# Attention and channel mix on one core: value loads on 128 partitions, products by even and odd key blocks, five turned batches, four loads in flight

## The chip, the cores and the metric

One core of a Trainium2 chip runs the whole kernel. The metric is the device time of one execution in microseconds, as the median of some runs. TensorE is called PE in the profile, VectorE DVE, ScalarE ACT, GpSimd POOL and SyncE SP.

## What is computed

Eight batches of causal attention, with 8 heads, 576 positions and 64 columns a head. The mask works by blocks of 64 positions, so query block i sees key blocks 0 to i whole. The heads' outputs, side by side, make x of 512 columns, which goes through a channel mix:

```python
attn = softmax(where(block_i >= block_j, q @ k.T / 8, -1e9));  x = heads_side_by_side(attn @ v)
x_prev = x shifted by one position
xk = mu_k * x + (1 - mu_k) * x_prev;  xr = mu_r * x + (1 - mu_r) * x_prev
out = sigmoid(xr @ w_r) * (relu(xk @ w_k) ** 2 @ w_v)
```

w_k is 512 x 1024, w_v 1024 x 512, w_r 512 x 512. Inputs and output are float32; the kernel computes products in 16 bits.

## The kernel before, in words

**Tasks and order.** The kernel first lists some 980 tasks, each with an engine, the tasks that it depends on and the buffers that it uses. Then it issues them in an order that is written out by hand: ORDER is a list of task numbers, and each engine works through its own tasks in that order, one after the other. A "+n" behind a number asks for n fills ahead of that task: matmuls of the identity (`unread`, L252, 128x512) whose result nobody reads, and which keep TensorE busy while it would wait. PLACE says, with one letter for each task that may go to several engines, which one takes it. Both texts are replaced by the change.

**Loads and their queue.** SP issues all transfers in its own order: loads (`load`, L224), turns (L349) and stores (L824). A transfer that has to wait holds all that stand behind it. Loads of float32 go into a ring of seven buffers (`ld`) and are cast to 16 bits on POOL, DVE or ACT (`convert`, L235 to L243).

**q and k.** Scores need q and k with the 64 columns of a head on partitions. In the first batches ("long", LONGS = 4: batches 0 to 3), a load brings two heads by two (`longld`, runs of 2,304 bytes, 576 KB a load; halves in batch 0). After the cast (`long`), TensorE transposes (`qt`, L302, 18 transposes of 64x64 a task, 8 tasks a batch, written into one bank of PSUM by both halves of the array), and ACT or DVE copies the result to SBUF (`ev`, 4 a batch). In the later batches a load brings 128 positions by 64 columns (`qkld`, in two pieces of 288 KB, runs of 256 bytes), and after the cast (`qk`) a transposing transfer (`turn`, L349) writes the turned form; there are four turns a batch, and all four must have landed ahead of the first scores.

**Attention.** `sc b gi` computes a unit of scores, keys on partitions: 12 units a batch, 14 in batch 0. Each unit writes a buffer of ring `s` in PSUM (three buffers of two banks). `ex` (ACT, L458) takes the exponential into ring `e`. Half u of the partitions holds the heads 4u to 4u + 3; c counts the four heads in a half. Then `av` multiplies by the values with column tiles of 32 and row tiles of 64: task S adds up the exponentials by a matrix of ones, `pick` (L488), A and B give the even and the odd columns of the output (L497, 72 matmuls each), T the first 64 queries (16 matmuls, into the same PSUM buffer as S). The order was S, T, A, B or another mixture; none waits for another. In A and B, row half u always writes bank u. DVE turns the sums (`t1`, L531), takes reciprocals (`rec`) and spreads them (`t2`), and `norm` (L560, L552) multiplies each product by them into x. Batch 0 goes through attention in two parts (L591, L596), the first 256 queries ahead; there A and B of the first part lie in one buffer, X.

**Values.** `vld b g` loads 64 positions on partitions: heads 0 to 3 on partitions 0 to 63 and heads 4 to 7 on 64 to 127, as two transfers of 64 partitions each (288 KB, runs of 256 bytes). `v` casts them to ring `vo`.

**Mix.** `d` (POOL or DVE) subtracts neighbours, `mul` (DVE, L686) makes xk and xr. In chunks of 512 positions, `pk` (L733) multiplies by w_k, `relu` and `sq` square it, `pr` (L768) multiplies by w_r, `tanh` stands for the sigmoid, `pv` (L799) multiplies by w_v, and `o` (DVE, L811) makes the output in a ring of two `o` buffers, whose `store` goes out through SP. pk, pr and pv share a ring of two banks (`mm`).

Of the kernel before, what the change touches and what calls it, by code (L numbers as in the profile page):

```python
# [9 lines left out]
F16 = mybir.dt.float16  # L10
# [4 lines left out]
LONGS = 4  # L15

ORDER = """
# [54 lines left out]
    "PPDDPDPPDDPPPAAPDAAAAAADPPDDDDPPDAPPDDADAADDPPPPAPPPDAAAPPDDDAPDAA"  # L72
    "ADDDDDDDPAPAPPPDDPDDDPDPDDDDDAAADDDDDPPDPDDDPPDDAAAPDPDPAPDPAADAAA"
    "DADADADADPAPAPDDAPADAADAAAADAADPDDAPAPAPAADAAAADDAAAAPAAAPDAAAAAAA"
    "DDAAAADPAAAPADDPADADAPADAAAPADADADAPAAAPAPADADAPAPADAPAPADAA")
# [56 lines left out]
def kernel(  # L132
# [64 lines left out]
    pick = consts.tile([P, QC], F16)  # L197
# [9 lines left out]
    for u in range(2):  # L207
        nc.vector.memset(
            pick[u * D:u * D + D, u * QC // 2:(u + 1) * QC // 2], 1.0)
# [3 lines left out]
    tiles, cast, evac = {}, {}, {}  # L213

# [5 lines left out]
    def load(key, dst_key, buf, jobs):  # L220
        def fn(eng, me):
            tiles[dst_key] = new(buf)
            for dst, src in jobs(tiles[dst_key]):
                nc.sync.dma_start(dst, src)  # L224
        return add(key, "SP", fn, uses=[buf])
# [95 lines left out]

    def add_cross(b):
# [5 lines left out]
        for g in range(2):  # L328
            for n, src in enumerate((q, k)):
# [4 lines left out]
                             (d[:, x].rearrange("p (i c) -> p i c", c=D),  # L334
                              src[b, 4 * g + 2 * x:4 * g + 2 * x + 2]
                              .rearrange("h s c -> (h s) c").rearrange(
                                  "(i p) c -> p i c", p=P))
# [23 lines left out]
    def operand(b, it, y, x, n):  # L361

        at = (it + 2 * y if b < LONGS else 2 * y + it) * S
        return new(qkt_buf[b])[x * D:x * D + D, n, at:at + S]

    def values(b):
        return new(vo_buf[b])[:, :].rearrange(
            "p (c t d) -> p c t d", c=4, d=D)

    def add_v(b):  # L370
        for g in range(2):
            vl = plan.buf("ld")
            t = load(f"vld {b} {g}", ("vl", b, g), vl, lambda d, g=g: [
                (d[u * D:u * D + D].rearrange("p x (t d) -> p (x t) d", d=D),
                 v[b, 4 * u + 2 * g:4 * u + 2 * g + 2].rearrange(
                     "x (t p) d -> p (x t) d", p=D))
                for u in range(2)])

            def fn(eng, me, g=g):
                convert(eng, new(vo_buf[b])[:, 2 * S * g:2 * S * (g + 1)],  # L380
                        tiles["vl", b, g][:, :].rearrange("p x c -> p (x c)"))
            cast["v", b, g] = flex(f"v {b} {g}", ANY, fn, [t],
                                   uses=[vl, vo_buf[b]])

# [50 lines left out]
    def add_scores(b, it):  # L435
# [5 lines left out]
        def fn(eng, me):  # L441
            PS = new(m)
            unread(me, PS[:, 0])
            for col, t, q0, n in UNITS[b][it[1]]:
                for y in range(2):
                    for x in range(2):
                        nc.tensor.matmul(  # L447
                            PS[y * D:y * D + D, x, col:col + n],
                            operand(b, it[0], y, x, 1)[:, t * D:t * D + D],
                            operand(b, it[0], y, x, 0)[:, q0:q0 + n],  # L450
# [14 lines left out]
    def weight(vals, kind):  # L465
        f = "AB".index(kind)
        return values(vals[0])[vals[1], vals[2], vals[3]].rearrange(
            "p (c f) -> p f c", f=2)[:, f]

    HALF = S // 2  # L470

    def blocks(b, PA, kind):

        for t in ([JT] * (kind in "ST") + [*range(JT)] * (kind != "T")):
# [3 lines left out]
            for c in range(GH):  # L480
# [3 lines left out]
                if kind == "S":  # L484
                    for y in range(2):
                        a, z = max(lo, y * HALF), min(lo + n, (y + 1) * HALF)
                        if a < z:
                            nc.tensor.matmul(  # L488
                                PA[out, y, a - y * HALF:z - y * HALF], pick,
# [4 lines left out]
                for u in range(2):  # L494
                    rows = slice(u * D, u * D + D)
                    for f in range(2) if kind == "T" else ("AB".index(kind),):
                        nc.tensor.matmul(  # L497
                            PA[out, u, HALF + f * D:HALF + f * D + D]
                            if kind == "T" else PA[out, u, lo - D:lo - D + n],
                            weight((b, rows, c, t % JT), "AB"[f]),  # L500
                            E[rows, bank, at:at + n],
                            start=t in (0, JT), stop=t >= JT - 1)

    def add_av(b):
# [3 lines left out]
        vals = [cast["v", b, g] for g in range(2)]  # L508
# [4 lines left out]
        for kind in "STAB":  # L513
            tail = kind == "T"

            def fn(eng, me, kind=kind):
                PA = new(m[kind])
                unread(me, PA[:, 0])
                blocks(b, PA, kind)
# [390 lines left out]
```

## Time and profile before

| what | value |
|---|---|
| median of 3 runs | 264.09 us (264.03 to 264.37) |
| the profiled execution | 266.22 us |
| its span, from first to last instruction | 264.4 us |
| mean clock granted to TensorE | 0.992 |
| HBM read, written | 33.56 MB, 9.44 MB |
| packets of the data queue q1 | 106,432, of which 95,040 under 512 bytes |
| SP: store L824 waited for DVE (o) | 72.2 us in total |
| ACT: exponentials waited for scores | 21.3 us in total |

The page of the profile gives busy times by engine, a view in 40 slices of the span (a digit is the busy share in tenths), the DMA queues, the chain of work that ended last, followed back from the end, and groups of instructions by line. The trace answers finer questions: who waited for whom, the chain in order of time, the busy time in chosen windows, the queue of SP. A line of the chain has its start in us, its length in us, the engine, the tile that it writes, the line of the kernel and the number of instructions. A line of a window has the window, its length, then for PE, PEld, DVE, ACT and POOL the busy time and the number of instructions, then the clock granted to TensorE, the DMA share and GB/s.

### The profile page before, as it was taken

To read this page: it belongs to the slowest core of one execution; us is meant where nothing else is said; L and a number is where in the kernel's file an instruction comes from. 1 tells how busy PE (TensorE), PEld (TensorE's weight loads), DVE (VectorE), ACT (ScalarE), POOL (GpSimd) and SP (SyncE) were. 2 spreads that over 40 slices of the span, in tenths; PEclk is the share of its full clock that TensorE was granted. 3 is DMA by queue.
4 is the path that set the end of the run, shared out by engine and by line. 5 is a ranking of instruction groups with operands and counts; after the bars stand their busy time and mean duration, and the time that the engine had idled before them with its cause. 6 is when DMAs were issued, how large, how long until landed. Compare 5 with 4: busy or idle time off the path is not lost.

```text
span 264.4 us, 8844 instructions
## 1 busy us (share of the span) xinstructions
PE 249.4 (94%) x3916; PEld 127.2 (48%) x3916; DVE 182.7 (69%) x270; ACT 178.8 (68%) x241; POOL 71.7 (27%) x71
## 2 busy tenths in 40 slices
PE   7899677996999999999999999979999999999994
PEld 3555346764446444554554455435544464444452
DVE  0448636889497987799858968957699578743332
ACT  1779587893799689598499855976688540472530
POOL 3215544442407511122144013001310324130410
PEclk9999999999799999999999999999999999999999
DMA  7999999399999999999789999999602200300403
GB/s 227 275 250 390 389 202 319 119 333 206 214 195 299 205 151 263 243 191 198 154 225 197 178 227 190 188 258 218 154 0 82 79 5 26 134 2 0 159 21 139
DMA packets 106470, 48.28 MB, mean 183 GB/s; under 512 B 95040, under 2 KB 95296, under 8 KB 106432
## 3 DMA queue, kind: packets, MB, share of 16 engines
q1 hardware_dynamic: 106432, 47.72, 79.1%
q8 instruction: 30, 0.49, 0.9%
q14 instruction: 8, 0.07, 0.1%
HBM read 33.56 MB, written 9.44 MB: 163 GB/s over the span
## 4 chain that ended last, share of the span: by engine, by line
PE 91%; issue 3%; ACT 2%; DMA 2%; DVE 1%; POOL 0%; SPq 0%; POOLq 0%; DVEq 0%; ACTq 0%
PE t_mm L733 24%; PE t_mm L799 24%; PE t_mm L768 11%; PE t_s L447 9%; PE t_s L497 7%; PE t_mm L252 6%; PE t_s L302 4%; PE t_s L488 4%; DMA out_dram<-t_o 2%; PE t_s L596 1%; ACT t_e L458 1%; PE t_s L591 1%; ACT t_qkt L235 0%; DVE t_o L811 0%; ACT t_kr L744 0%
## 5 line engine op out<-in xcount | busy, mean ns | idle before, releaser
L458 ACT ACTIVATE t_e<-t_s 128x1024 f16<-128x1024 f32 (+3 forms) x98 | 88.5, 957 | 21.6 <-PE t_s L447 21.3
L733 PE MATMUL t_mm<-t_xk,WK 128*128 128x512 f16 (+1 forms) x320 | 68.9, 358 | 1.4 <-issue 1.4
L799 PE MATMUL t_mm<-WV,t_k 128*128 128x512 f16 (+1 forms) x296 | 67.2, 380 | 1.6 <-DVE t_o L811 1.6
L755 POOL TENSOR_TENSOR t_k<-t_kr 128x512 f16<-128x512 f32 x27 | 29.6, 1104 | 101.6 <-ACT t_kr L744 55.3
L744 ACT ACTIVATE t_kr<-t_mm 128x512 f32<-128x512 f32 x53 | 31.5, 598 | 22.3 <-PE t_mm L733 21.6
L799 PEld LDWEIGHTS <-t_k 128*128 128x128 f16 x296 | 28.6, 99 | 35.6 <-issue 4.4
L733 PEld LDWEIGHTS <-WK 128*128 128x128 f16 x320 | 29.3, 98 | 31.6 <-issue 5.3
L811 DVE SCALAR_TENSOR_TENSOR t_o<-t_t,t_mm 128x512 f32<-128x512 f32 (+1 forms) x37 | 24.8, 671 | 22.7 <-PE t_mm L799 17.9
L768 PE MATMUL t_mm<-WR,t_xr 128*128 128x512 f16 x144 | 35.8, 380 | 0.2 <-ACT t_kr L744 0.2
L778 ACT ACTIVATE t_t<-t_mm 128x512 f32<-128x512 f32 x36 | 21.6, 601 | 15.7 <-PE t_mm L768 15.4
L447 PE MATMUL t_s<-t_qkt 64*64 64x512 bf16 (+7 forms) x680 | 30.0, 283 | 0.7 <-ACT t_qkt L235 0.7
L686 DVE SCALAR_TENSOR_TENSOR t_xr<-t_d,MUR,t_xt 128x576 f16<-128x576 f32 (+4 forms) x44 | 28.0, 650 | 2.4 <-POOL t_d L664 2.3
L686 DVE SCALAR_TENSOR_TENSOR t_xk<-t_d,MUK,t_xt 128x576 f16<-128x576 f32 (+4 forms) x44 | 29.2, 686 | 0.2
L241 POOL CAST t_nl<-t_ld 128x1152 bf16<-128x1152 f32 (+1 forms) x17 | 18.0, 1071 | 39.6 <-DMA t_ld<-in_k_dram 20.6
L447 PEld LDWEIGHTS <-t_qkt 64*64 64x64 bf16 x680 | 14.6, 106 | 17.3 <-issue 13.0
L755 DVE TENSOR_TENSOR t_k<-t_kr 128x512 f16<-128x512 f32 x17 | 13.3, 793 | 12.6 <-ACT t_kr L744 12.4
L753 ACT ACTIVATE t_k<-t_kr 128x512 f16<-128x512 f32 x28 | 17.2, 630 | 6.2 <-PE t_mm L799 6.0
L768 PEld LDWEIGHTS <-t_xr 128*128 128x128 f16 x144 | 13.0, 98 | 16.3 <-issue 2.8
L252 PE MATMUL t_mm<-identb 128*128 128x512 bf16 x59 | 17.4, 410 | 3.6 <-issue 2.2
L497 PE MATMUL t_s<-t_e,t_vo 64*32 64x512 f16 (+7 forms) x1120 | 20.6, 284 | 0.0
L664 POOL TENSOR_TENSOR t_d<-t_xt 128x576 f32<-128x576 f32 (+2 forms) x13 | 14.3, 1108 | 22.7 <-DVE t_xt L552 10.8
L560 DVE TENSOR_TENSOR t_xt<-t_s,t_rt 128x1024 f32<-128x1024 f32 x14 | 17.1, 1222 | 4.8 <-PE t_s L497 4.3
(47 smaller groups left out, 192.8 us busy)
## 6 DMA issues: line engine op xcount, KB each, us to landing
t_ld<-in_v_dram SPq DMA_DIRECT2D x32, 288.0 KB, 6.6
out_dram<-t_o SPq DMA_DIRECT2D x17, 512.0 KB, 3.6
t_ld<-in_q_dram SPq DMA_DIRECT2D x20, 288.0 KB, 5.4
t_ld<-in_k_dram SPq DMA_DIRECT2D x20, 288.0 KB, 5.1
t_ld<-in_k_dram SPq DMA_DIRECT2D x6, 576.0 KB, 7.0
t_ld<-in_q_dram SPq DMA_DIRECT2D x6, 576.0 KB, 6.4
t_ld<-in_moe_w_k_dram SPq DMA_DIRECT2D x4, 512.0 KB, 9.1
t_ld<-in_moe_w_v_dram SPq DMA_DIRECT2D x4, 512.0 KB, 6.4
```

The source lines that it names most:

```text
L252: nc.tensor.matmul(spare.get("at", dst), identb, identb[:, :].unsqueeze(1).to_broadcast([P, 4, P]), start=True, stop=True)
L447: nc.tensor.matmul(PS[y * D:y * D + D, x, col:col + n], operand(b, it[0], y, x, 1)[:, t * D:t * D + D], operand(b, it[0], y, x, 0)[:, q0:q ...
L458: nc.scalar.activation(new(ebuf)[:, :, 0:w], new(m)[:, :, 0:w], AF.Exp, scale=ISQ)
L497: nc.tensor.matmul(PA[out, u, HALF + f * D:HALF + f * D + D] if kind == "T" else PA[out, u, lo - D:lo - D + n], weight((b, rows, c, t % JT ...
L686: nc.vector.scalar_tensor_tensor(around[name][:, cc, at:at + w], new(d)[:, lo:lo + w], (MUK1, MUR1)[n][:, cc:cc + 1], x, ALU.mult, ALU.add)
L733: nc.tensor.matmul(ps[:, n], WK[:, cc, jc * P:(jc + 1) * P], xk[:, cc, lo:lo + w], start=(cc == 0), stop=(cc == CCn - 1))
L744: nc.scalar.activation(new(kr), new(m), AF.Relu)
L755: (nc.vector if eng == "DVE" else nc.gpsimd).tensor_tensor(dst, KR, KR, ALU.mult)
L768: nc.tensor.matmul(new(m), xr[:, cc, jt * P:(jt + 1) * P], WR[:, cc], start=(cc == 0), stop=(cc == CCn - 1))
L778: nc.scalar.activation(new(tb), new(m), AF.Tanh, scale=0.5)
L799: nc.tensor.matmul(new(m)[:, 0:w], k2[:, jc, jt * P:(jt + 1) * P], WV[:, jc, lo:lo + w], start=(jc == 0), stop=(jc == JCn - 1))
L811: nc.vector.scalar_tensor_tensor(new(o)[:, u, lo:lo + w], new(tiles["tbf", c, jt])[:, lo:lo + w], 1.0, new(m)[:, 0:w], ALU.add, ALU.mult)
```

## The change

- **Turned batches.** LONGS is 3: batch 3's q and k are now loaded in 256-byte runs and turned by transfers; its eight `qt` and four `ev` tasks go, four `turn` tasks come.
- **Values.** A value load brings 128 positions on partitions by blocks of 64 columns, two heads in a piece, as q and k are loaded in later batches. So a key block t of head c in half u stands on the upper or the lower 64 partitions by whether 9c + t + u is even. The load of the second half begins one block earlier, and the last block of head 7 of each batch, which no piece holds, comes for all batches by one more load (`vtld`) and cast (`vt`).
- **Products.** Row tiles must match the partitions of the values. So the scores of block t write the half that its values have (in `add_scores`, `u = y ^ t & 1 ^ ...`), and `pick` gets a second form for the odd blocks. An output is now added up by one row half over even blocks and by the other over odd blocks. `av` is split accordingly: A multiplies all even blocks (both column sets), then S, then T, then B with all odd blocks. S waits for A, T for `t1` (the turned sums of S), B for T, and all norms but T's for B. In batch 0 the first part too has A, S and B, with A and B in two buffers; B waits for `t1` and begins with one small matmul of 128 rows.
- **Loads in flight.** From the 13th to the 48th load transfer, a load waits until the fourth before it has landed.
- **Order.** ORDER and PLACE are new: 973 tasks, and 63 fills instead of 60. Batch 1's q and k are loaded ahead of batch 0's values. No task changes its sizes but as told.

```diff
-LONGS = 4
+LONGS = 3
...
+                ins = nc.sync.dma_start(dst, src).ins
+                if 12 <= len(sent) < 48:
+                    tc.add_manual_dep(
+                        ins, sent[len(sent) - AHEAD].name,
...
+                sent.append(ins)
...
+    def tiles_of(d, src, first):
+        return (d.rearrange("p (i c) -> p i c", c=D),
+                src.rearrange("b h s c -> (b h s) c")[
+                    first:first + 2 * S].rearrange("(i p) c -> p i c", p=P))
...
-                (d[u * D:u * D + D].rearrange("p x (t d) -> p (x t) d", d=D),
-                 v[b, 4 * u + 2 * g:4 * u + 2 * g + 2].rearrange(
-                     "x (t p) d -> p (x t) d", p=D))
-                for u in range(2)])
+                tiles_of(d[:, x], v, (b * H + 4 * g + 2 * x) * S - D * g)
+                for x in range(2)])
...
+                        u = y ^ t & 1 ^ (x if b < LONGS else it[0])
...
-    def weight(vals, kind):
+    def weight(b, u, c, t, kind):
+        at = JT * c + t + u
+        lo = at % 2 * D
+        if at == 4 * JT:
+            w = VT[0:D, b]
+        else:
+            at = (2 * JT * u + at // 2) * D
+            w = new(vo_buf[b])[lo:lo + D, at:at + D]
...
+    HALVES = {"A": [*range(0, JT, 2)], "B": [*range(1, JT, 2)]}
...
-        for kind in "STAB":
+        for kind in "ASTB":
...
+                for f in "AB" if kind == "A" else "BA":
+                    blocks(b, new(m[f]), f, HALVES[kind])
+            if kind == "A":
+                deps = [ready["x", b, pr, i] for pr in range(2)
+                        for i in (0, 2, 4)]
+            if kind == "S":
+                deps = exps + [av["A"]]
+            if kind == "T":
+                deps = first + [add_t1()]
+            if kind == "B":
+                deps = exps + [av["T"]]
...
-            done = add(f"norm {b} {kind}", "DVE", norm, [av[kind]] + t2s,
+            done = add(f"norm {b} {kind}", "DVE", norm,
+                       [av["T" if kind == "T" else "B"]] + t2s,
```

More of the change, by code (lines that the diff above doesn't have):

```diff
@@ L383, in add_v, with add_v_last, fn @@
                                    uses=[vl, vo_buf[b]])
+    def add_v_last():
+        vl = plan.buf("ld")
+        t = load("vtld", "vt", vl, lambda d: [
+            (d[0:D, 0, 0:CH].rearrange("p (b c) -> p b c", c=D),
+             v[:, H - 1, CH:S].rearrange("b p c -> p b c"))])
+        def fn(eng, me):
+            convert(eng, VT, tiles["vt"][0:D, 0, 0:CH].rearrange(
+                "p (b c) -> p b c", c=D))
+        cast["vt"] = flex("vt", ANY, fn, [t], uses=[vl])
     def add_w(name):
@@ L494, in blocks @@
                 for u in range(2):
-                    rows = slice(u * D, u * D + D)
                     for f in range(2) if kind == "T" else ("AB".index(kind),):
+                        rows, w = weight(b, u, c, t % JT, "AB"[f])
                         nc.tensor.matmul(
@@ L499, in blocks @@
                             if kind == "T" else PA[out, u, lo - D:lo - D + n],
-                            weight((b, rows, c, t % JT), "AB"[f]),
-                            E[rows, bank, at:at + n],
-                            start=t in (0, JT), stop=t >= JT - 1)
+                            w, E[rows, bank, at:at + n],
+                            start=t in (0, JT), stop=t in (JT, HALVES["B"][-1]))
     def add_av(b):
@@ L507, in add_av @@
         first = [ready["x", b, pr, 5] for pr in range(2)]
-        vals = [cast["v", b, g] for g in range(2)]
+        vals = [cast["v", b, g] for g in range(2)] + [cast["vt"]]
         ebufs = [tiles["ebuf", b, it] for it in its]
@@ L574, in add_av_part, with products @@
         span = (range(len(EARLY)), range(len(EARLY), len(UNITS[b])))[part]
[L575 to L576 removed]
+        pieces = sorted(((t, q0 - q_lo, i, col, n) for i in span
+                         for col, t, q0, n in UNITS[b][i]),
+                        key=lambda piece: (piece[0] % 2, piece))
         its = [(pr, i) for pr in range(2) for i in span]
         exps = [ready["x", b, pr, i] for pr, i in its]
[L579 removed]
+        vals = [cast["v", b, g] for g in range(2)] + [cast["vt"]]
         ebufs = [tiles["ebuf", b, it] for it in its]
[L581 to L582 removed]
+        m = {kind: plan.buf("s") for kind in "SAB"}
         av = {}
[L585 removed]
+        def products(f, t, at, n, i, col):
             for c in range(GH):
@@ L594, in products @@
                 for u in range(2):
-                    rows = slice(u * D, u * D + D)
-                    nc.tensor.matmul(
-                        PA[out, u, at:at + n], weight((b, rows, c, t), f),
-                        E[rows, c % 2, col:col + n], **flags)
-        for kind in kinds:
-            def fn(eng, me, kind=kind):
-                PA = new(m[kind])
-                unread(me, PA[:, 0])
-                for f in "AB" if kind == "X" else kind:
-                    for t, lo, i, col, n in pieces:
-                        products(PA, f, t, lo + W * (kind + f == "XB"), n,
-                                 i, col)
-            av[kind] = add(
-                f"av {b} {part} {kind}", "PE", fn,
-                exps + (vals if kind != "S" else []),
-                uses=[m[kind]] + ebufs
-                + ([vo_buf[b]] if kind != "S" else []))
@@ L614, in add_av_part, with fn, t1 @@
-        tt, rc, rt = plan.buf("d"), plan.buf("rc"), plan.buf("rt")
+                    rows, w = weight(b, u, c, t, f)
+                    nc.tensor.matmul(new(m[f])[out, u, at:at + n], w,
+                                     E[rows, c % 2, col:col + n], **flags)
+        tt, rc, rt = plan.buf("d"), plan.buf("rc"), plan.buf("rt")
+        for kind in "ASB":
+            def fn(eng, me, kind=kind):
+                if kind != "B":
+                    unread(me, new(m[kind])[:, 0])
+                else:
+                    nc.tensor.matmul(
+                        new(m["S"])[0:QC, 0, CH - QC:CH], pick[:, 0],
+                        new(ebufs[0])[:, 0, 0:QC], start=True, stop=True)
+                for f in {"S": "S", "A": "AB", "B": "BA"}[kind]:
+                    for t, lo, i, col, n in pieces:
+                        if kind == "S" or t in HALVES[kind]:
+                            products(f, t, lo, n, i, col)
+            deps = exps + (vals if kind != "S" else [])
+            if kind != "A":
+                deps.append(t1m if kind == "B" else av["A"])
+            av[kind] = add(
+                f"av {b} {part} {kind}", "PE", fn, deps,
+                uses=([m["S"]] if kind != "A" else [])
+                + ([m["A"], m["B"], vo_buf[b]] if kind != "S" else [])
+                + ebufs)
+            if kind == "S":
+                def t1(eng, me):
+                    nc.vector.transpose(new(tt)[:, 0:W],
+                                        new(m["S"])[:, 0, 0:W])
+                t1m = add(f"t1 {b} {part}", "DVE", t1, [av["S"]],
+                          uses=[tt, m["S"]])
@@ L615, in add_av_part @@
         NB = W // QC
-        def t1(eng, me):
-            nc.vector.transpose(new(tt)[:, 0:W], new(m["S"])[:, 0, 0:W])
-        t1m = add(f"t1 {b} {part}", "DVE", t1, [av["S"]], uses=[tt, m["S"]])
         def rec(eng, me):
```

118 lines of the change are left out of this document (57 added, 61 removed), and 102 rows, old and new, of the table ORDER.

## The prediction, made blind

> **What bounds the kernel now.** First the page's busy times and slices: which engine is full, and when.
>
> ```profile
> span 264.4 us, 8844 instructions
> PE 249.4 (94%) x3916; PEld 127.2 (48%) x3916; DVE 182.7 (69%) x270; ACT 178.8 (68%) x241; POOL 71.7 (27%) x71
> ...
> PE   7899677996999999999999999979999999999994
> ...
> DMA  7999999399999999999789999999602200300403
> ...
> q1 hardware_dynamic: 106432, 47.72, 79.1%
> q8 instruction: 30, 0.49, 0.9%
> ```
>
> TensorE is nearly never idle after slice 10, and the data queue (q1) is full until slice 28. So two things may bound, and I keep a ledger of TensorE. Its dense groups stand in the chain of waits: a pk or pr task 0.86 us (x4), a pv 1.73 (x8), a batch's sums 1.36 (x60), each half of its products 1.32 (x72), and scores of one batch some 2.8. Added up over the order, before needs 221.7 us of TensorE. The span has 264.4: 42.7 are lost. By the starts of the tasks in the trace, 22.4 are lost when pk 0 0 starts (36.5 us), 26.6 by 61.6 us, 31 by 75 us; then only about 0.35 per 5 us, until a step of 1.85 at 177 us; 3.3 are the tail. So the first 75 us hold most of what can be won. The chain of waits shows three of the pieces:
>
> ```profile
> 29.96 2.19 issue
> ...
> 61.58 0.30 PE t_s L302 x11
> 61.88 2.31 issue
> 64.20 1.80 PE t_s L302 x97
> ...
> 173.47 4.41 DMA out_dram<-t_o
> 177.98 0.70 DVE t_o L811
> ```
>
> "issue" is time without a wait that the profile shows. At 61.88 TensorE stops in the middle of one qt task (11 of its 18 transposes done), where no wait stands. The trace has a 16 KB packet of the instruction queue (q8) at 60.98 that took 1.46; at the stops at 29.96 and 44.80 (1.39 us) such packets started at 29.78 and 43.75. TensorE went on 1.3 to 1.8 us after each packet's end: I read these stops as TensorE running out of instructions, 5.9 us in all. The view by windows shows what followed the last one:
>
> ```profile
> 60.00:65.00 5.00, 2.69 (x70) 1.56 (x70) 5.00 (x8) 0.84 (x2) 0.77 (x1) 1.00 1.26 180
> 65.00:70.00 5.00, 5.00 (x86) 2.31 (x79) 3.35 (x4) 3.21 (x4) 3.00 (x2) 0.66 1.22 241
> ```
>
> The clock granted was 0.66 for 5 us: 1.7 us. The profiled execution took 266.22 (span 264.4 and 1.8 around it), the median of the runs is 264.09. I put 1.7 of those 2.1 down to that dip, and count it in no term: the sum below is a difference, taken from the median.
>
> The view of the DMA issues prices transfers:
>
> ```profile
> t_ld<-in_v_dram SPq DMA_DIRECT2D x32, 288.0 KB, 6.6
> ...
> t_ld<-in_q_dram SPq DMA_DIRECT2D x20, 288.0 KB, 5.4
> t_ld<-in_k_dram SPq DMA_DIRECT2D x20, 288.0 KB, 5.1
> ...
> t_qkt<-t_nl SPq DMA_TRANSPOSE x16, 4.6
> ```
>
> In a full queue, landings in the trace follow each other by 1.3 us (q, k pieces of 288 KB in 256-byte runs), about 1.45 (v pieces, the same runs on 64 partitions), 1.5 (576 KB of q, k in 2,304-byte runs), 1.35 (512 KB of weights or output) and 1.3 (a turn).
>
> **The change, part by part.**
>
> *Batch 3 turned by transfers.* Eight qt tasks go, 144 transposes: 36 in 0.57 (chain, 72.24) is 2.3 us, 97 in 1.80 is 2.7. They stood at 61 to 80 us, where TensorE is full: **-2.5**. Four ev tasks go (1.1 to 1.4 on ACT or DVE, neither full); the four casts stay. What is late next is the queue, below.
>
> *The stop at 61.88.* It fell in 108 transposes in a row, after 160 products, also short, and two pv. In the new order 72 transposes stand there after 80 products and two pv, and the other 80 products earlier, split off by pk and pr. Bounds: it stays (0) or goes (-2.3). **-1.5**, nearer to going, by the rows where such groups are short and no stop follows (36 transposes at 72.24). The Trainium skill, "Runtime: NRT & Kernel Launch", Instruction fetch mechanics, says fetch is hidden because instructions are issued more slowly than blocks are filled; three stops here speak against it. By that rule this term is 0 and the sum 261.7.
>
> *The start.* SP's new list: batch 0 (landed at 9.8 now), batch 1's q and k before v 0 (4 x 1.5: 15.8), v 0 (4 x 1.3: 21), its last block and mu (21.7), six weight loads (29.8). So the first values come 5 us later than now (15.9), but batch 1's transposes fill that time, and weights end as now (30.9). Then: cast 22.4, even products and sums 23.1, t1, rec, t2 (0.45, 0.25, 0.7) 24.6, two norms 26.1, the cast of weight k 1 (landed 27.4) 28.3, two differences 29.2, five muls of 0.48 31.6: pk 0 0 at about 32, with 11.3 of the ledger done, so 20.5 lost. Now it is at 36.5 with 14.1 done, 22.4 lost. From there to av 1 the new order has ten fills (2.2 us at 0.216; now one), and before loses 4.0 there, the stop of 1.39 among it. I take 24.0 for 26.4: **-2.4**; bounds +2 (all fills added to today's loss) and -5 (no loss beyond the fills).
>
> *Queue time.* Values: 32 pieces, 1.45 to 1.3: -4.8 (0 if the row's difference is the neighbours'). Batch 3: 8 pieces of 1.3 for 4 of 1.5, +4.4; four turns, +5.2; the last blocks +0.5. Net +5 over the run, and some +8 ahead of batch 4's turns, while the new order asks for batches earlier: first scores of batch 4 with 75.4 of the ledger done (now 79.8), of batch 7 with 142.9 (153.5). Up to its last turn the queue has 165 us at these rates. In 66 to 131 us 60.5 us of such rates took 65.4, so some 10 us of gaps come on top: 175, and TensorE is there at 142.9 + 24 + 1 + 4 = 172 to 173. **+2**; bounds 0 and +16 (all 24 us of gaps that the queue has now).
>
> *Four loads in flight.* From the 13th load, a load waits on SP until the fourth before has landed; behind it wait mu, weights, batch 3's turns. A landing takes 5.1 to 6.6 us at a spacing of 1.3 to 1.5, so about four are under way now. Bounds: 0, as 128 KB landed in 1.7 when nothing was ahead, and 36 x 0.3 = +11 if a landing still takes 6.6 with four. **0**, nearer to the first: most of 6.6 is queueing.
>
> *Even and odd blocks.* The products are the same in number and size (+2 small ones in batch 0). New waits: T waits for t1 (0.78 on DVE), B for T, both norms for B; behind T on TensorE stand B and the next pk. In six of seven batches two tasks (1.7 us) stand between S and T, once one (0.87): cover of 1.7 for 0.8 and DVE's queue. **+1**; bounds 0 and +5 (0.8 x 7 uncovered). Norm X as two costs DVE 0.4.
>
> *The store at 173.5.* DVE waited for an o buffer, as its store stood on SP behind a turn. In the new list store 3 1 1 stands behind a turn and two loads: **-0.5**, bounds 0 and -1.85.
>
> Casts and relus move between engines: by their rows ACT has 14 us less, DVE 2 more, POOL 13 more (it is 27% busy): 0.
>
> Sum: -2.5 - 1.5 - 2.4 + 2 + 0 + 1 - 0.5 = -3.9: **260.2 us**, 0.50 (256.5 to 263.5).
>
> **Rivals.**
>
> *All stops go.* With fewer instructions in a row all three vanish (-5.9), the transposes -2.5, a start otherwise 1 better: 254.7. For: each stop followed such a packet. Against: the start stays dense. 0.17.
>
> *The queue becomes the bound* (slower). From 136 to 190 us 48 us of rates took 54.6, 14% of gaps. At that, 165 becomes 182 or more at batch 7's last turn, TensorE stands 9 instead of 2: 267. It decides from 8 us of gaps on. For: the new order leaves 2 us where now a turn issued at 182 serves scores at 191. Against: some of today's gaps (50 to 54, 131 to 133 us) are SP waiting for buffers while ahead. 0.20.
>
> *The value load is no quicker* (the change doesn't do what it says): 4.8 us of queue stay, 4 of them show: 264.2. 0.06.
>
> *Halves of the array that write one bank.* Now row half u always writes bank u; afterwards heads of odd number do it crosswise, so both halves write one bank at a time, on other partitions. If that excluded each other, products would take twice as long: 2 x 1.32 x 7, and 3.2 in batch 0: +21.7, 282. Against it: the transposes (L302) have both halves in one bank, and 36 take 0.57, 16 ns each, where 64 columns alone take 27 (0.216 us per 512). 0.05. The Trainium skill, "TensorEngine Tiling (Array Packing)", Gotcha 1: PSUM Pressure, states this rule: different row tiles cannot access the same bank simultaneously. By it the sum is 282; the transposes speak against it.
>
> 0.02 are left for other losses.
>
> **Numbers.** Measurement tells about 0.2% from no change: 263.6 to 264.6. Faster 0.67, same 0.06, slower 0.27. The range goes from 254.5 (stops gone) to 267.5 (queue), leaving out the crosswise banks, the worst of the queue and the best of the start.
>
> **What would show it.** Right: no L302 after batch 2's, no issue stop near 60 us, pk 0 0 by 33 us, v landings at q's, TensorE busy from 75 us on. Wrong: TensorE waiting for t_qkt ahead of a batch's first scores (queue), 72 products in more than 1.5 us (banks), idle time between S and T (t1), or pk 0 0 after 36 us.

## The result, and the profile after

The kernel after takes **274.16 us** (272.04 to 279.43) where before, in the same call, takes 264.23: ratio 1.0336, 95% interval 1.0248 to 1.0424. It is slower by 9.9 us by the medians, and by 8.9 by the ratio, which leaves out one execution of after (279.43) that ran slow at a lower granted clock (0.975). The forecast was 260.2, and the time lies above the range. The profiled execution of after took 272.04, 2.1 below its median, and that of before 266.22, 2.0 above its own, so the two traces show 5.8 us of difference; the rest lies between one execution and the next, and no trace here holds it.

The page of after, the rows that answer to those shown of before (busy times, then the 40 slices, then the queues):

```profile
span 270.2 us, 8588 instructions
PE 252.3 (93%) x3777; PEld 125.0 (46%) x3777; DVE 186.2 (69%) x277; ACT 166.9 (62%) x224; POOL 86.8 (32%) x81
...
PE   7999579999999899699999999969999999999994
...
DMA  7997999999999999999999999999000400400403
...
q1 hardware_dynamic: 119952, 49.04, 78.5%
```

The first row says most. TensorE runs 139 matmuls less than before (3777 for 3916), and yet is busy 2.9 us longer (252.3 for 249.4). The rest of the span, in which it is idle or the span has not begun or ended with it, also grew by 2.9 (17.9 for 15.0). So the 5.8 us are half work and half waiting. Split at the start of pk 0 0 (36.5 us in before, 35.0 in after), the records say where: ahead of it TensorE's busy time fell from 32.0 to 28.2 us and its idle time grew by 2.3; behind it busy time grew from 217.5 to 224.2 and idle time by 0.6. What moved across that point cancels: 8 matmuls of the mix and 125 of the sums and products came behind it (some 4.0 us), and 216 transposes less stand there (3.9). The slices show dips at 30 us (the 5), and at 90, 110 and 180 us.

The view of TensorE's waits has, for before (who waited for whom, us in total, times, longest):

```profile
PE t_s L302 <- issue: 2.6, 2, 2.3
PE t_mm L252 <- issue: 2.2, 1, 2.2
...
PE t_mm L733 <- issue: 1.4, 1, 1.4
```

That is 6.2 us for "issue"; 1.7 at a fill for ACT and 1.6 at pv for `o` come on top. After has:

```profile
PE t_mm L789 <- ACT WK L246: 3.3, 1, 3.3
PE t_mm L789 <- DVE t_o L867: 2.8, 3, 2.3
PE t_s L471 <- DVE t_xr L742: 1.4, 1, 1.4
...
PE t_mm L855 <- POOL t_k L811: 1.0, 1, 1.0
...
PE t_s L530 <- DVE t_d L549: 0.7, 1, 0.7
```

The list changed in kind. Before, TensorE stopped mostly at "issue"; after, no issue stop is left in this list, and real producers stand there instead: weights (3.3), an `o` buffer whose store is late (2.8), batch 4's scores (1.4), `sq`, and `t1`. The third row of after needs care: it names DVE's t_xr (ended 113.92), but a score needs no t_xr. It needs batch 4's turns, and the last of them landed at 113.89; the score began at 113.94.

The DMA issues of after (KB each, median us from issue to landing):

```profile
t_ld<-in_v_dram SPq DMA_DIRECT2D x32, 288.0 KB, 5.1
...
t_ld<-in_k_dram SPq DMA_DIRECT2D x24, 288.0 KB, 5.1
```

The value load does what it says: 5.1 us for 6.6, as fast as k's. That is not the limit's doing: the same row has 5.1 in after without the limit (`after_no_limit`), and 6.4 and 6.3 in before with the limit (`before_limit`, `before_limit_again`). In the old order the new load took 5.7 (`old_order_values`) and 5.5 (`old_order_all`).

### The profile page after: what moved, and what is told of

Read it like the earlier page. It is cut to its first block, busy times and chain, and to the rows that moved or that the text cites. A ratio compares the mean times of both kernels' runs of the same rounds, so it can differ in the third digit from the quotient of the medians.

```text
span 270.2 us, 8588 instructions
## 1 busy us (share of the span) xinstructions
PE 252.3 (93%) x3777; PEld 125.0 (46%) x3777; DVE 186.2 (69%) x277; ACT 166.9 (62%) x224; POOL 86.8 (32%) x81
## 4 chain that ended last, share of the span: by engine, by line
PE 57%; DMA 20%; DVE 9%; SPq 4%; issue 4%; POOL 3%; ACT 1%; POOLq 0%; DVEq 0%; ACTq 0%
PE t_mm L855 19%; PE t_mm L789 18%; PE t_mm L824 8%; DMA t_ld<-in_q_dram 8%; PE t_s L530 5%; PE t_s L471 5%; DMA t_ld<-in_moe_w_v_dram 5%; SPq L228 3%; DMA t_ld<-in_moe_w_k_dram 3%; DMA out_dram<-t_o 2%; PE t_s L520 2%; DVE t_xk L742 2%; DMA t_ld<-in_v_dram 2%; POOL t_nl L252 2%; DVE t_xr L742 2%
## 5 line engine op out<-in xcount | busy, mean ns | idle before, releaser
L482 ACT ACTIVATE t_e<-t_s 128x1024 f16<-128x1024 f32 (+2 forms) x98 | 89.0, 958 | 24.0 <-PE t_s L471 22.1
L789 PE MATMUL t_mm<-t_xk,WK 128*128 128x512 f16 (+1 forms) x320 | 70.8, 361 | 6.2 <-ACT WK L246 3.3
L811 POOL TENSOR_TENSOR t_k<-t_kr 128x512 f16<-128x512 f32 x28 | 31.7, 1143 | 64.5 <-ACT t_kr L800 41.9
L800 ACT ACTIVATE t_kr<-t_mm 128x512 f32<-128x512 f32 x46 | 27.3, 599 | 16.9 <-PE t_mm L789 15.7
L720 POOL TENSOR_TENSOR t_d<-t_xt 128x576 f32<-128x576 f32 (+2 forms) x17 | 21.9, 1289 | 42.0 <-DVE t_xr L742 20.8
L252 POOL CAST t_nl<-t_ld 128x1152 bf16<-128x1152 f32 (+1 forms) x19 | 20.5, 1090 | 43.8 <-DMA t_ld<-in_k_dram 18.3
L471 PE MATMUL t_s<-t_qkt 64*64 64x64 bf16 (+7 forms) x680 | 31.7, 284 | 3.0 <-DVE t_xr L742 1.4
L742 DVE SCALAR_TENSOR_TENSOR t_xr<-t_d,MUR,t_xt 128x576 f16<-128x576 f32 (+4 forms) x44 | 32.2, 747 | 0.0
L802 DVE TENSOR_SCALAR t_kr<-t_mm 128x512 f32<-128x512 f32 x26 | 17.9, 688 | 18.3 <-PE t_mm L789 15.7
L530 PEld LDWEIGHTS <-t_vo 64*32 64x32 f16 x1106 | 14.2, 92 | 11.0 <-issue 7.4
```

The source lines that it names most:

```text
L252: e.tensor_copy(dst, src)
L471: nc.tensor.matmul(PS[y * D:y * D + D, x, col:col + n], operand(b, it[0], u, x, 1)[:, t * D:t * D + D], operand(b, it[0], u, x, 0)[:, q0:q ...
L482: nc.scalar.activation(new(ebuf)[:, :, 0:w], new(m)[:, :, 0:w], AF.Exp, scale=ISQ)
L530: nc.tensor.matmul(PA[out, u, HALF + f * D:HALF + f * D + D] if kind == "T" else PA[out, u, lo - D:lo - D + n], w, E[rows, bank, at:at + n ...
L720: (nc.vector if eng == "DVE" else nc.gpsimd).tensor_tensor(new(d)[:, q_lo:q_hi], x[:, cc, 1 + q_lo:1 + q_hi], x[:, cc, q_lo:q_hi], ALU.sub ...
L742: nc.vector.scalar_tensor_tensor(around[name][:, cc, at:at + w], new(d)[:, lo:lo + w], (MUK1, MUR1)[n][:, cc:cc + 1], x, ALU.mult, ALU.add)
```

## The experiments

Ratios are to the kernel before in the same call, with their 95% intervals. The kernel after was timed in the first call alone, so its relatives are compared by ratio; its own interval is 1.8% wide, and a relief of less than about 1% can't be told from none. The prediction had put what can be told at 0.2%, from three runs; over the later calls the kernel before took 260.5 to 266.1 us. The "ledger" in the expectations is the prediction's: TensorE work done, by dense durations. Words in capitals there (START, QUEUE, ORDER) are names of theories, told in the expectations.

### The limit of loads in flight, alone

`after_no_limit` takes it out of after, `before_limit` and `before_limit_again` put it into before (both the same kernel).

```diff
-                if 12 <= len(sent) < 48:
-                    tc.add_manual_dep(ins, sent[len(sent) - AHEAD].name, ...
```

> The changed kernel without the wait for the fourth load before; all else as it is. Theory START (the wait leaves the queue short of work while the weights load: 264 GB/s at 20 to 30 us, where before moves 393): the weights land 3 us earlier, pk 0 0 starts at 32 instead of 35 us, and the time falls by 3 to 6 us, to 268 to 271. Theory QUEUE (batch 3's turned transfers are what delays batch 4 by 8 us): the start gains 1 to 2 us at most, 272 to 274. Theory ORDER (the new order itself): within 1 us of 274.

> The kernel before, with the wait added alone: from its 13th load transfer to its 48th, a load waits until the fourth before has landed. START: the weights land 2 to 4 us later and the kernel is 2 to 5 us slower, 266 to 269. QUEUE and ORDER: no difference, within 1 us of 264.2.

> The kernel before with the limit of four loads in flight alone, timed in more rounds than in its first run, where the ratio stayed open. If the limit is worth what its one profile shows (the store's wait of 1.6 us gone, three stops of TensorE shorter by 3.3 together), the ratio to the kernel before is 0.985 to 0.995, below 1 with its whole interval. If that profile was a lucky execution, the interval holds 1.

after_no_limit: 274.04, ratio 1.0440 (1.0374 to 1.0506), so the limit is not what is slow. before_limit: 260.87 against 261.91, no ratio settled, but not the 266 to 269 of START. before_limit_again: 261.19, ratio **0.9909 (0.9867 to 0.9951)**: the limit alone makes the old kernel faster, and this version beats both kernels. Its span is 256.4; its busy times and its waits for issue:

```profile
PE 248.0 (97%) x3916; PEld 126.8 (49%) x3916; DVE 182.0 (71%) x270; ACT 179.2 (70%) x241; POOL 69.7 (27%) x71
```

```profile
PE t_s L506 <- issue: 1.5, 1, 1.5
...
PE t_mm L742 <- issue: 0.6, 1, 0.6
PE t_mm L261 <- issue: 0.4, 1, 0.4
PE t_s L311 <- issue: 0.3, 1, 0.3
```

Issue stops are 2.8 us in all where before has 6.2, and the wait for `o` is gone. (This profiled execution, 258.18, is 3 us below its own median, so it flatters; that of before_limit, 260.01, has 2.8 too.)

### Batch 3 turned, in the old order

`before_turn3`: LONGS = 3 in before, its turns where loads had stood. `turn3_early`: with the limit, and batch 3's loads, casts and turns ahead of batch 4's loads. `after_long3` goes the other way: after with batch 3 transposed on TensorE again, the eight tasks put between batch 2's scores.

```diff
-LONGS = 4
+LONGS = 3
```

> The kernel before with LONGS = 3 alone: batch 3's q and k come in 256-byte runs and are turned by four transfers, at the places in the order where its loads stood and shortly after; its qt and ev tasks are left out of the order. QUEUE: 10 us more of transfers ahead of batch 4 make TensorE wait there, 3 to 6 us slower, 267 to 270, less the 2.5 us of transposes. START and ORDER: the transposes go at no cost, 261 to 263.

> The kernel before with the limit and batch 3 turned by transfers, but its loads, casts and turns now stand ahead of batch 4's loads in the order. QUEUE (the queue has no room for 10 us more): still 4 to 9 us slower than before, 266 to 271, TensorE waiting at batch 3 or 4. ORDER (the run before lost its 11 us by the place of the turns alone): 257 to 261, the 2.5 us of transposes won.

> The changed kernel with LONGS = 4: batch 3 is loaded in long runs and transposed by TensorE again, its qt tasks put between batch 2's scores; everything else as it is. QUEUE: batch 4's last turn lands 8 us earlier, 4 to 7 us are won back less 2.5 of transposes, 269 to 272. START and ORDER: 2.5 us slower for the transposes, about 276.

before_turn3: 273.0, ratio 1.0423 (1.0364 to 1.0482), slower than any theory had it. turn3_early: 270.27, ratio 1.0298 (1.0221 to 1.0376), against 0.9909 for the same kernel with batch 3 transposed. TensorE's longest wait, first of before_turn3, then of turn3_early:

```profile
PE t_s L446 <- DMA t_qkt<-t_nl: 5.9, 1, 5.9
```

```profile
PE t_s L455 <- DMA t_qkt<-t_nl: 7.0, 1, 7.0
```

This is the rival "queue" in its pure form, but at batch 3's scores, not at batch 7's: in turn3_early TensorE stood ready for them at 77.4 us, and the last of the turns landed at 84.3. after_long3 missed: 280.92, ratio 1.0743 (1.0673 to 1.0813). Its queue was partly idle from 80 to 100 us (DMA shares of 0.63 and 0.37 there): SP issued nothing from 83 to 96 us, as a load waited 12.6 us for a buffer that a cast on POOL still held. So the order no longer fitted, and the run says nothing of the turns' price.

### Values and split products, in the old order

`old_order_values`: before's order and four transposed batches, with the new value load and with A, S, T, B. `old_order_all`: batch 3's turns and the limit as well.

```diff
-        for kind in "STAB":
+        for kind in "ASTB":
```

> The value loads on 128 partitions, the last blocks' load and the split products alone, in the order of before: batch 3 stays long, no limit. A and S stand where S stood, T two tasks later where the old order allows, B where the last product stood; tasks that lack a buffer move back. Theory PRODUCTS (T behind t1, B behind T, three PSUM buffers held at once cost TensorE time): 3 to 8 us slower, 265 to 270. QUEUE: values come quicker, 0 to 4 us faster, 258 to 262. ORDER: within 2 us of before, 260 to 264.

> All parts of the change (limit, values, products, batch 3 turned early as in turn3_early), in the order of before as far as it goes. ORDER: 258 to 264, some 10 us faster than the changed kernel with its own order. PRODUCTS or QUEUE: 268 to 276, as slow as the changed kernel.

286.61, ratio **1.0872 (1.0770 to 1.0973)**; and 294.23, ratio 1.1231 (1.1156 to 1.1306). Both are far slower than any theory had them (270 and 276 at most). Two of the waits of old_order_values:

```profile
PE t_s L462 <- DVE t_xt L606: 6.4, 5, 1.5
PE t_s L462 <- ACT t_e L473: 4.0, 4, 1.1
```

L462 is a score, L606 the norm of T. Scores wait for an accumulator: A fills both output buffers and S the third, and none comes free before T's norm or B, so ring `s` has nothing for scores meanwhile. The prediction had looked at the waits of T and B, but not at the buffers that they hold. The new order answers to this: between A and B it has mix tasks and hardly a score. It wins back most of 12.3%, but not all.

### The start

`after_values_first` asks for batch 0's values ahead of batch 1's q and k. `after_weights_order` changes the order of the weights:

```diff
-wld k 3, wld r 1, wld r 0, wld k 1, wld k 2, wld k 0
+wld k 1, wld k 0, wld r 1, wld r 0, wld k 3, wld k 2
```

> The changed kernel with batch 0's value loads ahead of batch 1's q and k, as before has them; all else as it is. Theory START in its second form (the new order of the first loads costs 4 us up to batch 1's products): batch 0's products start at 17 to 19 instead of 23 us, pk 0 0 stays near 33 as weights come no earlier: 1 to 3 us faster, 271 to 273. QUEUE and PRODUCTS: within 1 us of 274.

> The kernel after with the weights in another order on SP: k 1, k 0, r 1, r 0, k 3, k 2 (it has k 3, r 1, r 0, k 1, k 2, k 0), and their casts moved with them. START (the first 35 us are late because DVE waited from 27.06 to 31.34 for w k 1 and ACT until 33.9 for w k 0): pk 0 0 starts at 31.5 to 33 us instead of 35.0, and the time falls by 2 to 3.5 us. WAITS: pk 0 0 comes earlier, but the next tasks wait for differences, muls and the norms of batch 0's second part, which DVE makes in turn; the ledger's loss at pk 0 5 (29.5) stays within 1 us, and so does the time.

In after the chain of waits shows the start held by w k 1 and, behind it on DVE, by all that pk 0 0 needs:

```profile
23.30 8.01 DMA t_ld<-in_moe_w_k_dram
...
31.34 0.69 DVE WK L252
32.03 0.67 DVE t_d L720 x2
...
33.09 0.87 DVE t_xk L742 x3
```

pk 0 0 began at 35.0. after_values_first missed: 276.69, ratio 1.0553 (1.0473 to 1.0633), pk 0 0 at 41.1, as TensorE then waited 5.9 for batch 1's cast. In after_weights_order pk 0 0 began at 33.3, short of the 33 expected at most, and the ratio is 1.0341 (1.0279 to 1.0402): no gain, but 1.7 us are also less than the runs can tell. The trace shows the 1.7 us lost again by batch 4: its first scores started at 114.0, at 113.9 in after, as the second theory said. (Its profiled span still ends 1.8 us earlier, 268.4; there pk waits 0.5 us for `o` where after waits 2.8.)

### Batch 4's place, and the store

`after_batch4_first` asks for batch 4's last piece and turns ahead of pieces of 5 and 6; `after_three_orders` adds the weights' order and moves a store ahead of a turn; `after_orders_pool` keeps batch 4's casts on POOL.

```diff
-qkld 4 1 0, vld 3 1, store 0 1 1, store 0 3 1, qkld 5 0 0, turn 4 1 0, qkld 6 1 1, turn 4 0 1, qkld 4 1 1, ...
+qkld 4 1 0, qkld 4 1 1, vld 3 1, store 0 1 1, store 0 3 1, turn 4 1 0, turn 4 0 1, turn 4 1 1, turn 4 0 0, qkld 5 0 0, ...
```

> The kernel after with one stretch of SP's list reordered: batch 4's last piece and its four turns are asked for ahead of the first pieces of batches 5 and 6; two casts of batch 4 go to ACT. QUEUE (what is late from 94 us on is late because batch 4's turns stand behind other batches' pieces): batch 4's last turn lands by 107 us (113.9 in the kernel after), TensorE's idle 1.43 at 112.5 goes, and the time falls by 1.5 to 3 us from the kernel after's. WAITS (the loss there is that of T behind t1 and of three accumulators held): the turns come earlier, the idle times at 91.9 and 109.7 stay, and the time falls by less than 1 us. Should batch 5's turns (141.1 last) become late in their place, the time does not fall at all.

> The kernel after with batch 4's pieces and turns ahead, the weights in the other order, and the store of 3 1 1 moved ahead of a turn (it stood behind a turn and two loads). ORDER (each of the three places is a loss of its own: 3 at the start, 2 to 3 at batch 4, 2 at the store): 266 to 268 where the kernel after takes 274, still not below the kernel before. WAITS: the losses come back a little later, since T, B and the accumulators set the pace from 80 us on; 271 to 274.

> after_three_orders with the two casts of batch 4 on POOL instead of ACT. There ACT stood from 85 to 90 us in a cast that waited for its piece, with a tanh behind it that held an accumulator (the ledger's step of 4.2 at 92 us). QUEUE: that step goes with the cast, but turns behind pieces that come late show later: 270 to 272. If the order alone was to blame: 266 to 268.

Ratios 1.0441 (1.0367 to 1.0516), 1.0389 (1.0311 to 1.0467), 1.0442 (1.0380 to 1.0504): none is faster than after. Batch 4's last turn landed at 103.0, 102.4 and 105.0 instead of 113.9, and its first scores still began at 114.5, 115.8 and 119.2. What came in place of the turn is seen in after_three_orders:

```profile
PE t_mm L824 <- ACT t_t L834: 4.0, 1, 4.0
```

ACT stood in a cast that waited for its piece, and the tanh behind it held an accumulator of `mm`. On POOL the cast holds up `sq` instead: in after_orders_pool pv waits 1.9 us for it at 95 us. The expectation of 270 to 272 failed.

### Less queue, and T without t1

`after_no_values` and `before_no_values` leave out the value loads of batches 2 to 7; `after_free_t1` lets t1 read ones, so that T waits for nothing on DVE.

```diff
-                for x in range(2)])
+                for x in range(2 if b < 2 else 0)])
```

```diff
-                    new(m["S"])[:, :, 0:HALF])
+                    ONES)
```

> The kernel after without the value loads of batches 2 to 7 (24 pieces of 288 KB, about 31 us of queue; their casts read what stands in the buffers, so the output is not the reference's from batch 2 on). All instructions of the engines stay. QUEUE (the 8 us lost more than before lie with late pieces and turns, wherever the list puts them): the steps at 82, 94, 110, 116 and 182 us go, the ledger ends near 38 lost instead of 47: 262 to 265. WAITS (T behind t1, B behind T, three accumulators held): 270 or more.

> The control: the kernel before without the value loads of batches 2 to 7 (24 pieces of 288 KB), its output likewise not the reference's. QUEUE: before was bound by TensorE from 75 us on and has little to win: 2 to 4 us less, 258 to 261, so that the two kernels without these loads stand within 4 us of each other, where they are 9 to 10 apart with them. WAITS: both win the same few us, and the gap of 9 to 10 stays.

> The kernel after with t1 of batches 1 to 7 transposing a buffer of ones instead of the sums (the output is not the reference's: the softmax is not divided by its sums). T then waits for nothing on DVE, and t1 not for the sums. WAITS: 0.5 to 1 us each in six or seven batches: 267 to 270 where the kernel after takes 274. QUEUE: less than 1.5 us.

269.69, ratio 1.0259 (1.0202 to 1.0316); 260.79, ratio 0.9910 (0.9872 to 0.9947); 274.75, ratio 1.0412 (1.0332 to 1.0492). With 24 pieces off the queue the two kernels still stand 8.9 us apart, so the queue's load is not what divides them (269.69 lies between the two forecasts, by QUEUE 262 to 265, by WAITS 270 or more). T's wait for t1 costs nothing that can be measured, where 267 to 270 had been expected. In after_free_t1 scores wait for turns instead, of batches 3 and 4 by the landings; at batch 4 after had waited 1.4:

```profile
PE t_s L473 <- DMA t_qkt<-t_nl: 5.0, 2, 2.8
```

The spans of before_no_values and after_no_values are 261.1 and 269.3; their busy times:

```profile
PE 249.4 (96%) x3916; PEld 127.9 (49%) x3916; DVE 183.9 (70%) x270; ACT 179.1 (69%) x241; POOL 71.6 (27%) x71
```

```profile
PE 253.6 (94%) x3777; PEld 125.5 (47%) x3777; DVE 187.5 (70%) x277; ACT 167.1 (62%) x224; POOL 87.5 (32%) x81
```

Again half of the 8.2 us between them, 4.2, is TensorE's own busy time.

### All reliefs at once, and TensorE's own work

`after_relieved` joins no values, free t1, the weights' order, batch 4 ahead and the store. `before_split_scores` is before_limit_again with 15 more places where a score is followed by a matmul of the full array:

```diff
-sc 4 02, sc 4 15, sc 4 14, pr 2 3
+sc 4 02, sc 4 15, pr 2 3, sc 4 14
```

> The kernel after with all the single reliefs together: no value loads from batch 2 on, t1 of batches 1 to 7 reading ones, the weights in the other order, batch 4's pieces and turns ahead (casts on POOL), the store ahead of a turn. Its output is not the reference's. MASKED WAITS (each wait hides the next one, so that one alone is worth 0 to 4.6 us and all together more than their sum of about 7): 262 or less. OWN WORK (TensorE itself has more to do in the new order, waits or not): its idle time goes but it stays busy for 252 to 254 us, 266 to 268.

> The kernel before with the limit, and with the last score of 15 groups of scores in batches 4 to 7 moved behind the next task of the full array, so that there are 15 more places where a score is followed by a matmul of the full array. Nothing else moves. OWN WORK: the last score of a group stands in the records 0.3 us longer than one that is followed by another score, which overlaps it on the other half of the array; 15 of them cost 2.5 to 4.5 us, and TensorE's busy time grows by that: 264 to 266 where before_limit_again took 261.2. MASKED WAITS: such a switch costs nothing by itself: 260 to 262.5.

after_relieved: 266.44, ratio **1.0118 (1.0058 to 1.0178)**, inside 266 to 268 and far from 262: the masked waits don't hold the whole. They hold a part: together the reliefs bring 2.2%, where the largest alone, no values, brought 0.8%. Against before_no_values (0.9910), which has as little queue, 2.1% are left. Its span is 266.8:

```profile
PE 253.3 (95%) x3777; PEld 124.8 (47%) x3777; DVE 186.3 (70%) x278; ACT 167.0 (63%) x224; POOL 85.5 (32%) x81
```

Of the 5.7 us between the two spans, 3.9 are busy time (253.3 for 249.4).

before_split_scores: 264.49, ratio 1.0027 (0.9983 to 1.0071) against 0.9909, about 3.1 us for 15 switches, some 0.2 us each, inside the 264 to 266 of "own work". Its span is 262.7, its busy times:

```profile
PE 252.6 (96%) x3916; PEld 125.7 (48%) x3916; DVE 183.4 (70%) x270; ACT 178.8 (68%) x241; POOL 70.9 (27%) x71
```

And the group of the scores in before_limit_again, before_split_scores and after (busy us, then mean ns):

```profile
L456 PE MATMUL t_s<-t_qkt 64*64 64x512 bf16 (+7 forms) x680 | 30.0, 283 | 0.7 <-ACT t_qkt L244 0.7
```

```profile
L456 PE MATMUL t_s<-t_qkt 64*64 64x512 bf16 (+7 forms) x680 | 33.0, 285 | 0.7 <-ACT t_qkt L244 0.7
```

```profile
L471 PE MATMUL t_s<-t_qkt 64*64 64x64 bf16 (+7 forms) x680 | 31.7, 284 | 3.0 <-DVE t_xr L742 1.4 <-ACT t_e L482 1.1 <-DVE t_xt L607 0.2
```

The mean of one score is the same (283 to 285 ns), but the union of 680 of them is 30.0, 33.0 and 31.7 us: scores run on quarters of the array and overlap one another, and the last of a group has nothing to overlap with. Counted until the next matmul starts, a score takes 0.03 us where another score follows, 0.04 to 0.06 where a transpose does, and 0.19 to 0.21 where a matmul of the full array does. By the traces, a matmul of the full array (pk, pr, pv or a fill) follows a score at 37 places in before, 52 in before_split_scores and 49 in after; 8 of the 12 more in after are fills.

## Why the prediction was wrong

From the records of the traces, each matmul counted until the next one starts or it ends itself (us):

| kind | before | before_limit_again | before_split_scores | after | after_relieved |
|---|---|---|---|---|---|
| transposes | 11.0 | 10.8 | 10.7 | 8.1 | 8.1 |
| scores | 25.3 | 25.3 | 27.2 | 27.7 | 28.0 |
| fills | 16.3 | 16.3 | 17.1 | 17.4 | 18.3 |
| sums and products | 33.7 | 34.0 | 34.6 | 35.0 | 35.3 |
| pk, pr, pv | 163.1 | 161.6 | 163.0 | 164.0 | 163.7 |
| all | 249.4 | 248.0 | 252.6 | 252.3 | 253.3 |

**The sum** is the step that failed first. It took the transposes off and left TensorE's other work as it was, at dense durations. The transposes did go (2.9 for my 2.5), but scores cost 2.4 more, the fills 1.1, the sums and products 1.3 and the mix 0.9. (The traces of before and after have 5 us each at a granted clock of 0.66. By an estimate from the records it costs pv and transposes 1.7 in before, and in after the mix 0.8 and batch 0's sums 0.8; without it the sums and products cost 0.5 more and the mix 1.7.) So busy time is +2.9 instead of -2.5, 5.4 of the 9.7 by which the two traces miss the forecast difference. That an order has prices of its own at the ends of groups was in no term; before_split_scores shows such a price, about 0.2 us a switch (0.13 in the scores' own row), and 12 switches more in after make 1.5 to 2.4, most or all of what its scores cost more. The fills are three more (63 for 60), ten of them behind pk 0 0 for one, and those ten (2.7) the start's term had counted; why fills take 18.3 in after_relieved (0.4 of it by the low clock there) was not tried, and neither was why the products and the mix cost more.

**The start**, -2.4, is the second. I had the weights land by 30.9 as before; that was the fifth of the six in before (the last landed at 33.8), and in after the last landed at 33.9. The chip moved 264 GB/s from 20 to 30 us where before moved 393, and w k 1, which DVE waits for, landed at 31.3 instead of the 27.4 in my sum (31.6 without the limit, so the limit did not hold it). pk 0 0 came at 35.0 for my 32; 23.7 us of the ledger were lost there for my 20.5. An earlier start alone gave back nothing that the runs can tell, though (after_weights_order), so this term was wrong in size and perhaps in what it is worth.

**Queue time**, +2: the sum looked at batch 7 and had both sides early: its last turn landed at 185.05 for my 175, but TensorE came to its first scores only at 187.5 for my 172 to 173 (before at 190.9), so it had no wait there. The place that decides came earlier: batch 3 in the old order (7 us), batch 4 in the new one (turns at 113.9). The prediction had the extra 8 us ahead of batch 4's turns and did not check them against batch 4's first scores. With these turns landed at 95.5 (after_relieved) the scores began at 110.7, 3.2 us earlier, which is the most that can be theirs: the other reliefs have their part in it, and the turns' landing at 103.0 alone (after_batch4_first) moved the scores not at all. The rival "the queue becomes the bound" was right on the sign, wrong in its place, and by after_no_values not the main cause.

**Even and odd blocks**, +1: T's wait for t1 is 0.7 in the trace, and after_free_t1, which takes it away, is no faster, so that term was at most what it was put at. But the three accumulators held from A to B were missing. In the old order the split and its loads cost 8.7%; the new order buys this off, and more switches are part of what it pays. How much of after's loss is this, and not the order's other moves, is open: it was not separated.

**The stop at 61.88**, -1.5: gone, and all others in after's profile too, as the rival "all stops go" said (in after's relatives some come back, 2.6 in all in after_values_first); 6.2 us of issue waits vanished, and waits for producers came in their place. The sum of TensorE's waits is 12.1 for 10.4 (without the first fill's).

**Four loads in flight**, 0: it is worth 0.9% in before, and nothing that the runs can tell in after. **The store**, -0.5: it waited longer (2.8 in all for 1.6), as store 3 1 1 was issued at 175.45 and landed after 6.24:

```profile
175.45 6.24 DMA out_dram<-t_o
...
181.82 0.70 DVE t_o L867
```

**Halves that write one bank**: no. The chain has the even and odd products at the old rate, 18 and 19 ns a matmul (72 in 1.32 before):

```profile
101.67 1.43 PE t_s L530 x80
...
114.27 1.21 PE t_s L530 x64
```

The Trainium skill, "TensorEngine Tiling (Array Packing)", Gotcha 1: PSUM Pressure, says that different row tiles cannot use one bank at the same time; the trace disagrees for tiles that write different partitions of it, as the unchanged rate shows no exclusion. **Value load no quicker**: no, 5.1 for 6.6. It can have brought little: even 24 of the 32 loads left out are worth 0.9% in before and 0.8% in after.

What stays open: of the 2.1% between after_relieved and before_no_values, 1.5% is busy time, spread over scores, fills, products and mix, and a run of its own stands only behind the scores; the rest, and what the profiled pair doesn't show of the loss, have no cause here.

## What to carry to other kernels

Where TensorE is 94% busy and a change brings a new order, compare the busy total before any wait: the dense duration of a task is not its price at a group's end, and scores on quarters of the array want company of their own kind. Price a split of an accumulation by the buffers that it holds, not by the waits that it adds, and try each part in the old order, which shows the price before a new order hides it. Waits taken away one to three at a time showed no gain that could be told in five kernels here; where the traces were read (after_free_t1, after_three_orders), another producer's wait had come in their place.

## What the runs showed of the hardware

TensorE's stops at "issue" fall on a grid. The four stops of over 1 us of before between 29 and 62 us (one of them, of 1.65 us at 37.5, stands in the view of waits as one for ACT) come at matmuls 607, 735, 863 and 1247 of the trace, all 95 beyond a multiple of 128; with a weight load each, that is a grid of 256 instructions, and ahead of all four a 16 KB packet of the instruction queue had started, 0.2 to 1.2 us before (the prediction had read three such stops). The one stop of over 1 us in before_limit_again, 1.54 us at matmul 1119, lies on the same grid. The Trainium skill, "Runtime: NRT & Kernel Launch", Instruction fetch mechanics, gives blocks of 256 instructions, which agrees, and calls the crossing mostly hidden, which these four crossings were not. In the order of before, the issue waits were 6.2 us, and 5.5 in before_no_values; with no more than four loads in flight they were 2.8 (before_limit, before_limit_again) and 4.1 (before_split_scores). That a crowded data queue delays the instruction packets fits this, but no run shows it by itself.
